# A fused attention and GeGLU kernel: one query group moved into the next block, a query/key group as half-tile pairs, padding copies ahead of the masks, a last PV ahead of its gates

## The chip, the cores and the metric

The kernel runs on one core of a Trainium2 chip. The metric is the device time of one execution in microseconds (us); less is better.

## The reference

With S = 2048 rows, D = 448, 16 heads of 28 and F = 1792, in bfloat16:

```
xn  = layernorm(x)                                   # no scale, no shift
q, k, v = split(xn @ wqkv)                           # 16 heads of 28
o   = softmax(q k^T / sqrt(28), window of 256, causal) v
out = x + o @ wo + (gelu(xn @ w_gate) * (xn @ w_up)) @ w_down
```

A query sees itself and the 255 rows ahead of it.

## The kernel before, in words

The rows are worked in four blocks (`qb` 0 to 3) of 512. The order of every engine is the order in which the program writes its instructions; no scheduler changes it. Eight PSUM banks are shared out by hand: four for scores or gates, four (`b0` to `b3`) that `take` hands out and `give` puts back, first in, first out.

**A block** has two stages. The attention stage is a list of score steps (nine in block 0, ten in the others, `steps_of`, L473). A step writes `sc` (L600), ScalarE turns it into `p_sb` by an exponential of 1.88 us (L604), the window is masked (by GpSimd selects, L528, in block 0; by VectorE products with the `masks` tile, L518, later), and TensorE meanwhile does the filler that `plan` lists for that step (L747 to L767). A filler entry `(u, 7)` advances the generator `u` seven times; `"sums"` and `"inverse"` put the softmax's denominators on VectorE, and `scale_o` (L537, GpSimd) multiplies by them. Every few steps `pv` (L562) multiplies the masked scores with `v_sb`, for the four head groups `g` 0 to 3 in turn; the last, `pv(3)`, is called by `rest` (L627). The second stage, `gated` (L422), does the gate products (`gt`), their Gelu, and the up products (`u`, or `ue` where they were made earlier). Its `last_v` is `rest`: so `pv(3)` stands behind gate 0. Its `hook` starts later work: norms and transposes of rows to come, `collect` and `deliver`.

**Projections.** `proj` and `qk_halves` (L229, L233) make q and k of a group as three products of 128 rows each and one of 64 rows each. `gen_pairs` (L311) makes them as seven pairs of 64-row products, two on the array at once; half of the operands then have to be in the other 64 partitions, which is what the copies `xsw` (from `xnT`) and `wsq` (from the padded weights `wqp` and `wkp`, L385) are for. Block 0's three later groups come from `gen_qk` (L259).

**Group 3 of k** has, for blocks 1 to 3, no products of its own. The 32 columns of a head leave four columns of padding, and `fill_pads` (L276) writes the weights of the last four k heads there, by small GpSimd copies. Group 3 of q comes from `q_last` (L249), four 128-row products. `collect` (L299) then sends the padding rows of `qT` and `kT` to DRAM by eight DMAs, and `deliver` (L306) reads them into `kT` by four.

**Queues.** Nearly all DMAs are issued by SP in program order; SP waits where the source is not ready, and everything behind it waits too. The start of its list: loads, `swap(0)` for `xsw` (L680), rows 8 to 11 of x (L681), then in `ahead` (L707) the transpose of row tile 4, the weights `wvs` and a slice of `wu`; in `ahead3` (L720) three more transposes, the `xsw` copies of block 1 and the remaining weights. The two `wsq` copies are issued by ScalarE in step 3 of block 0.

`make_masks` (L109) is 18 GpSimd selects. It stands before block 0's attention, `fill_pads(False)` in its step 2. The final stage is block 3's down product (`po`, L359) and the output.

Of the kernel before, what the change touches and what calls it, by code (L numbers as in the profile page):

```python
# [16 lines left out]
S, D, H, Dh, F = 2048, 448, 16, 28, 1792  # L17
P = 128
# [8 lines left out]
def kernel(  # L27
# [11 lines left out]
    nc = tc.nc  # L39
# [233 lines left out]
            qk_copies(0, g, pq, pk)  # L273
            yield 360

    def fill_pads(last):  # L276


        def put(dst, src, n, lo):

            src = src.rearrange("p (j d) -> p j d", d=Dh)[:, :, lo:]
            if n == 4:
                nc.gpsimd.tensor_copy(out=dst[:, 12:16, Dh:32], in_=src[:, :, 24:28])
            src = src[:, :, 0:24].rearrange("p j (g i) -> p g j i", i=8)[:, :, :, 0:4]
            nc.gpsimd.tensor_copy(out=dst[:, 0:12, Dh:32].rearrange("p (g j) i -> p g j i", j=4), in_=src)

        if not last:
            for c in range(3):
                k = wraw[:, c, D + 12 * Dh:2 * D]
                put(wqp[:, c, :, :], k, 4, 0)  # L290
                put(wkp[:, c, :, :], k, 3, 4)
            return
        put(w3p[0:64, :, :], w3k[0:64, :], 4, 0)
        put(w3p[64:128, :, :], w3k[64:128, :], 3, 4)
        nc.gpsimd.memset(w3p[64:128, 12:16, :], 0.0)

    k3 = dram.tile([4, 7, 4, QB], bf16, name="k3")
# [87 lines left out]
    def swap_weights():  # L385

        for hi, src in enumerate((wqp, wkp)):
            nc.scalar.dma_start(out=wsq[64 * hi:64 * hi + 64], in_=src[64 - 64 * hi:P - 64 * hi, 0:3])

    def xchunk(qb, hi, c, t0, n):  # L390

# [30 lines left out]
    def gated(qb, early, last_v, flush, hook):  # L422

        hT = hTs[qb]
        us, ges = {}, {}

        def up(p):
            if p in early:
                return
            us[p] = [take("u") for _ in range(2)]  # L430
            for c in range(7):
                chunk(us[p], wu, p, qb, c)

        def gate(p):
            gt = phase[0].pool.tile([P, 2, QB], f32, name="gt", tag="s")
            for c in range(7):
                chunk([gt[:, i, :] for i in range(2)], wg, p, qb, c)
            if not p:
                last_v()
            ges[p] = work.tile([P, 4, QB], bf16, name="p_sb", bufs=5)[:, 0:2, :]  # L440
            nc.scalar.activation(out=ges[p][:, :, :], in_=gt[:, :, :], func=ACT.Gelu_apprx_tanh)  # L441

        def end(p):
            ge = ges.pop(p)
            if p in early:
                nc.vector.tensor_tensor(out=both(hT, p), in0=ge[:, :, :], in1=both(hT, p), op=ALU.mult)
            else:
                for i, u in enumerate(us.pop(p)):
                    nc.vector.tensor_tensor(out=hT[:, p + 7 * i, :], in0=ge[:, i, :], in1=u, op=ALU.mult)  # L449
                    give(u)  # L450
                    flush()
            hook(2 * p)

        up(0)
        gate(0)
        end(0)
        gate(1)
        if 1 in early:
            end(1)
            gate(2)  # L460
            up(2)
        else:
            gate(2)
            up(1)
            end(1)
            up(2)
        end(2)
        for p in range(3, 7):
            gate(p)
            up(p)  # L470
            end(p)
# [59 lines left out]
    def attention(qb, plan):  # L531
# [4 lines left out]
        def scale_o(g, oc, inv):  # L536
            nc.gpsimd.tensor_tensor(out=oN[:, g, :], in0=oc[:, :], in1=inv, op=ALU.mult)  # L537
# [24 lines left out]
        def pv(g):  # L562

            ov = [take("ov") for _ in range(2 if qb else 1)]
            todo = parts.pop(g)
            for n, (half, kt, q0, nq, col, p_sb) in enumerate(todo):
                k0 = 64 * half if half else 0
                r = slice(k0, k0 + (P if half is None else 64))
                for j in range(4):
                    nc.tensor.matmul(ov[half or 0][32 * j:32 * j + 32, q0:q0 + nq], lhsT=v_sb[r, kt, 4 * g + j, :],  # L570
                                     rhs=p_sb[r, j, col:col + nq], start=n == (half or 0), stop=n + len(ov) >= len(todo),
                                     tile_position=(k0, 32 * j), skip_group_check=True)
            oc = work.tile([P, QB], f32, name="oc", tag="wb" if g % 2 else "wa", bufs=1)
            if qb:
                if g > 1:
                    behind.append((oc, ov))
                else:
                    add_halves(oc, ov)
            else:
                (nc.scalar.copy if g == 1 else nc.vector.tensor_copy)(out=oc[:, :], in_=ov[0][:, :])  # L580
                give(*ov)
            copied.append((g, oc))
# [3 lines left out]
        for i, (scores, ncol, edges) in enumerate(steps):  # L586
# [24 lines left out]
            while later:  # L611
                scale_o(*later.pop(0))
            for n in plan[i]:
                if n == "sums":
                    sums()
                elif n == "inverse":
                    inverse()
                if not isinstance(n, tuple):
                    if callable(n):
                        n()  # L620
                    continue
                for _ in range(n[1]):
                    next(n[0], None)
            if qb == 3 and i - 2 in pvs:
                inverse()

        def rest():  # L627
            while fresh:
                apply_masks(*fresh.pop(0))
            if not qb:  # L630
                scale_o(*later.pop(0))
                sums()
                inverse()
                scale_o(*later.pop(0))
            pv(3)

# [41 lines left out]
    transp(3, nc.vector.tensor_copy, "b3")  # L678
    pads(nc.scalar.copy, wkp, slice(0, 1))
    swap(0)  # L680
    nc.sync.dma_start(out=x_sb[:, 8:12, :], in_=xv[:, 8:12, :])  # L681
    pvs.append(take("pv", D))
    v_dense(1, pvs[1])
    pvs.append(take("pv", D, "b2"))
    pq, pk = (phase[0].pool.tile([P, 2, QB], f32, name="s0", tag="s")[:, 0, :] for _ in range(2))
    proj(pq, wqp, 0, 0)
    proj(pk, wkp, 0, 0)
    nc.vector.tensor_copy(out=w3p[:, :, 0:Dh], in_=wraw[:, 3, 0:D].rearrange("p (h d) -> p h d", d=Dh))
    nc.vector.memset(masks[:, 0, 0, 0:1], 1.0)
    make_masks()  # L690
    stat(4)
    rstd(4, 1)
    stat(5)
# [11 lines left out]
        pads(nc.vector.tensor_copy, dst, slice(2, 4))  # L705

    def ahead():  # L707
        norm(4)
        dma_transp(4)
        wv64 = A_wqkv[0:3 * P, 2 * D:3 * D].rearrange("(c h p) n -> h p c n", h=2, p=64)  # L710
        for hi in range(2):
            nc.sync.dma_start(out=wvs[64 * hi:64 * hi + 64, :, :], in_=wv64[1 - hi])
        load_ffn(wu, B_w_up, slice(0, 1))
# [6 lines left out]
    def ahead3():  # L720
# [2 lines left out]
            dma_transp(t)  # L723
        swap(1, 4, 2)
        swap(1, 6, 2)
        fill_pads(False)
        load_ffn(wg, B_w_gate, slice(0, 3))
        nc.sync.dma_start(out=x_sb[:, 12:16, :], in_=xv[:, 12:16, :])
        load_ffn(wu, B_w_up, slice(4, 7))
# [7 lines left out]
    for qb in range(NB):  # L737
# [4 lines left out]
        if qb == 0:  # L742
            new_hT(0)
            early = (0, 1, 2, 3)
            u = chain(gen_qk((1, 2, 3), {1: (3, pvs[3]), 2: (2, pvs[2])}), gen_up(0, (1, 2, 3, 0), (3,)))
            w = gen_pairs(1, (("v", 0), ("v", 2), ("k", 0), ("k", 1), ("k", 2)))
            plan = [[(u, 2), ahead, (u, 1)], [lambda: v_dense(2, pvs[2]), (u, 2), ahead2, (u, 1)],  # L747
                    [lambda: spare.append(spare.pop(1)), (u, 2), ahead3, (u, 4)], [swap_weights, lambda: stat(8), (u, 11)],
                    [lambda: stat(9), (u, 7), lambda: stat(10), (u, 7), lambda: fill_pads(True)], [(w, 7), "sums", "inverse"],
                    [(w, 11)], [lambda: stat(11), (w, 6), lambda: rstd(8, 4)],  # L750
                    [lambda: q_last(1, nc.vector.tensor_copy), (w, 4), "sums", "inverse", (w, 7)]]
        else:
            d = gen_down(qb - 1)
            if qb < 3:
# [3 lines left out]
                if qb == 1:  # L758
                    for i in range(4):
                        plan[i].insert(0, lambda t=12 + i: stat(t))  # L760
                    plan[4].append(lambda: rstd(12, 4))
            else:
                new_hT(3)
                early = (1, 2, 3, 4, 5, 6)
                u = gen_up(3, early)
                plan = [[(d, 14)], [(d, 4), (u, 5)], [(u, 9)], [(u, 7)], [(d, 18)], [(u, 7)], [(d, 13)], [(d, 5), (u, 7)],
                        [(u, 7)], [(d, 18)]]  # L767
        if qb in (1, 2):
            swap(qb + 1)
        score_pool(1)  # L770
        rest, after, flush = attention(qb, plan)
        nc.scalar.preload_act_table(ACT.Gelu_apprx_tanh)
        score_pool(2)
        if qb not in hTs:
# [1 line left out]

        def hook(f):
            after(f)
            if qb < 3 and f == 4:
                collect(qb + 1)  # L780
            if qb < 3 and f == 10:
                deliver(qb + 1)
            t = ({0: 8, 4: 9, 8: 10, 10: 11} if qb == 0 else {4: 12, 6: 13, 8: 14, 10: 15} if qb == 1 else {}).get(f)
            if t is not None:
                norm(t)
                dma_transp(t)
# [155 lines left out]
```

## Time and profile before

| | us |
|---|---|
| median of 3 runs | 217.1 |
| lowest and highest | 216.55, 217.58 |
| profiled execution, its own time | 216.48 |
| its span | 214.6 |
| TensorE busy in the span | 208.7 |
| VectorE, ScalarE, GpSimd busy | 159.8, 130.7, 46.4 |

The span runs from the first to the last instruction; 1.88 us of the execution's own time lie around it. Times within the trace are counted from the span's start. The granted TensorE clock is 1.0 in the whole span. The chain of waits follows the last instruction back to what released it; the time of a row in it is what that piece added to the chain, so neighbouring rows can be summed. In the timeline a row's time is that of the instructions themselves, which overlap on TensorE.

### The profile page before, as it was taken

What the parts mean: (1) busy time and instruction counts of PE and PEld (TensorE: products, weight loads), DVE (VectorE), ACT (ScalarE), POOL (GpSimd) and SP (SyncE); (2) the same over time, 40 slices, a digit from 0 to 9 for tenths busy, and PEclk for the clock granted to TensorE, in tenths of its full rate; (3) what the DMA queues carried; (4) which work ended last, traced back from release to release, by engine and by line L of the source; (5) the groups of instructions that cost most, each with busy time, mean ns of one, the idle gap of its engine ahead of it and who ended that gap; (6) DMA issues with size and microseconds to landing.
All of it is one profiled execution on the core that took longest, in us unless ns stands there. A gap on an engine that the chain in (4) does not pass through costs nothing.

```text
span 214.6 us, 6346 instructions
## 1 busy us (share of the span) xinstructions
PE 208.7 (97%) x2722; PEld 101.1 (47%) x2722; DVE 159.8 (74%) x355; ACT 130.7 (61%) x122; POOL 46.4 (22%) x78
## 2 busy tenths in 40 slices
PE   6999999999999999999999999999999999999993
PEld 2433444444444444444445436544444444444892
DVE  7899987997776995698546899576449699587621
ACT  4699599554877976523777897432678576466000
POOL 5287658630000211022000202022000021114001
PEclk9999999999999999999999999999999999999999
DMA  6998789993240001002230000200000000000011
GB/s 187 275 245 152 159 194 244 226 290 77 60 106 5 20 3 32 17 15 59 50 95 24 24 3 0 62 5 3 0 24 3 23 3 24 21 3 2 23 35 39
DMA packets 24193, 15.21 MB, mean 71 GB/s; under 512 B 9856, under 2 KB 24032, under 8 KB 24160
## 3 DMA queue, kind: packets, MB, share of 16 engines
q1 hardware_dynamic: 23056, 14.08, 28.3%
q10 hardware_dynamic: 1104, 0.68, 1.3%
q8 instruction: 22, 0.36, 0.8%
q14 instruction: 11, 0.09, 0.1%
HBM read 9.03 MB, written 2.18 MB: 52 GB/s over the span
## 4 chain that ended last, share of the span: by engine, by line
PE 94%; DVE 2%; ACT 1%; DMA 1%; issue 1%; DVEq 0%; ACTq 0%
PE po L359 26%; PE gt L401 20%; PE u L401 13%; PE ue L401 7%; PE sc L600 6%; PE pq L333 6%; PE ov L570 5%; PE pv L319 4%; PE pq L190 2%; PE pv L190 1%; DMA x_sb<-in_A_x_dram 1%; ACT p_sb L604 1%; DVE st L154 1%; PE s L190 1%; PE pk L190 1%
## 5 line engine op out<-in xcount | busy, mean ns | idle before, releaser
L604 ACT ACTIVATE p_sb<-sc 128x2048 bf16<-128x2048 f32 x39 | 73.3, 1878 | 20.6 <-PE sc L600 15.3
L441 ACT ACTIVATE p_sb<-gt 128x1024 bf16<-128x1024 f32 x28 | 28.6, 1023 | 39.5 <-PE gt L401 32.6
L537 POOL TENSOR_TENSOR oN<-oc,l 128x512 bf16<-128x512 f32 x16 | 22.3, 1391 | 137.8 <-DVE l L550 137.8
L359 PE MATMUL po<-wd,hT 128*128 128x448 bf16 (+1 forms) x266 | 47.9, 324 | 0.0
L401 PE MATMUL gt<-xnT,wg 64*128 64x512 bf16 x224 | 45.4, 376 | 0.0
L401 PE MATMUL gt<-xsw,wg 64*128 64x512 bf16 x168 | 40.6, 376 | 0.0
L449 DVE TENSOR_TENSOR hT<-p_sb,u 128x512 bf16<-128x512 bf16 x36 | 23.3, 680 | 19.6 <-PE u L401 11.9
L518 DVE TENSOR_TENSOR p_sb<-p_sb,masks 128x256 bf16<-128x256 bf16 (+1 forms) x90 | 30.2, 389 | 5.0 <-ACT p_sb L604 5.0
L359 PEld LDWEIGHTS <-hT 128*128 128x128 bf16 x266 | 24.6, 98 | 16.0 <-issue 1.4
L401 PE MATMUL u<-xnT,wu 64*128 64x512 bf16 x144 | 29.9, 376 | 0.0
L401 PEld LDWEIGHTS <-wg 64*128 64x128 bf16 x392 | 19.3, 94 | 22.2 <-issue 0.2
L401 PEld LDWEIGHTS <-wu 64*128 64x128 bf16 x392 | 18.6, 94 | 23.2 <-issue 3.1
L401 PE MATMUL u<-xsw,wu 64*128 64x512 bf16 x108 | 26.1, 376 | 0.0
L367 DVE TENSOR_TENSOR res<-po,x_sb 128x448 bf16<-128x448 f32 (+1 forms) x17 | 10.1, 593 | 17.3 <-PE po L359 17.3
L401 PE MATMUL ue<-xnT,wu 64*128 64x512 bf16 x80 | 16.6, 377 | 0.0
L600 PE MATMUL sc<-qT,kT 28*64 28x320 bf16 (+7 forms) x648 | 16.4, 261 | 0.1
L528 POOL TENSOR_SCALAR_AFFINE_SELECT p_sb<-p_sb 128x512 bf16<-128x512 bf16 (+1 forms) x21 | 14.2, 701 | 6.5 <-ACT p_sb L604 6.4
L359 PE MATMUL po<-wo,oN 128*128 128x448 bf16 (+1 forms) x76 | 15.1, 323 | 0.0
L401 PE MATMUL ue<-xsw,wu 64*128 64x512 bf16 x60 | 14.9, 377 | 0.0
L600 PEld LDWEIGHTS <-kT 28*64 28x64 bf16 (+1 forms) x648 | 7.5, 102 | 12.6 <-issue 11.0
L418 DVE CAST hT<-ue 128x512 bf16<-128x512 f32 x19 | 12.1, 679 | 0.5 <-PE ue L401 0.4
L570 PE MATMUL ov<-p_sb,v_sb 64*32 64x320 bf16 (+7 forms) x648 | 11.7, 256 | 0.1
(103 smaller groups left out, 265.6 us busy)
## 6 DMA issues: line engine op xcount, KB each, us to landing
out_dram<-res SPq DMA_DIRECT2D x15, 112.0 KB
wd<-in_B_w_down_dram SPq DMA_DIRECT2D x2, 784.0 KB
x_sb<-in_A_x_dram SPq DMA_DIRECT2D x3, 448.0 KB
wu<-in_B_w_up_dram SPq DMA_DIRECT2D x4, 336.0 KB
xsw<-xnT SPq DMA_DIRECT2D x6, 192.0 KB
wg<-in_B_w_gate_dram SPq DMA_DIRECT2D x2, 448.0 KB
wg<-in_B_w_gate_dram SPq DMA_DIRECT2D x2, 336.0 KB
wraw<-in_A_wqkv_dram SPq DMA_DIRECT2D x2, 252.0 KB
```

The costliest lines, as they stand in the source:

```text
L333: nc.tensor.matmul(ps, lhsT=w.rearrange("p h d -> p (h d)"), rhs=xchunk(qb, hi, c, qb * QB, QB), start=c == 0, stop=c == 6, tile_position= ...
L359: nc.tensor.matmul(po[:, a:b], lhsT=x[:, k, cs], rhs=wt[:, k, lo + a:lo + b], start=(n == a == 0), stop=(n == len(terms) - 1), skip_group_ ...
L401: nc.tensor.matmul(ps, lhsT=w[64 * hi:64 * hi + 64, c, p * P:(p + 1) * P], rhs=xchunk(qb, hi, c, qb * QB, QB), start=c == 0, stop=c == 6, ...
L418: copy(out=hTs[qb][:, p + 7 * i, :], in_=us[i])
L441: nc.scalar.activation(out=ges[p][:, :, :], in_=gt[:, :, :], func=ACT.Gelu_apprx_tanh)
L449: nc.vector.tensor_tensor(out=hT[:, p + 7 * i, :], in0=ge[:, i, :], in1=u, op=ALU.mult)
L518: nc.vector.tensor_tensor(out=reg, in0=reg, in1=m, op=ALU.mult)
L528: nc.gpsimd.affine_select(out=reg, in_=reg, pattern=mid + [[1 if diag else -1, min(w, P)]], compare_op=ALU.is_ge, fill=0.0, base=0 if diag ...
L537: nc.gpsimd.tensor_tensor(out=oN[:, g, :], in0=oc[:, :], in1=inv, op=ALU.mult)
L570: nc.tensor.matmul(ov[half or 0][32 * j:32 * j + 32, q0:q0 + nq], lhsT=v_sb[r, kt, 4 * g + j, :], rhs=p_sb[r, j, col:col + nq], start=n == ...
L600: nc.tensor.matmul(ss[k0:k0 + nk, j, col:col + nq], lhsT=kT[r, g, kt * P + k0:kt * P + k0 + nk], rhs=qT[r, g, ring(qb).start + q0:ring(qb) ...
L604: nc.scalar.activation(out=p_sb[:, :, 0:ncol], in_=ss[:, :, 0:ncol], func=ACT.Exp, scale=SCALE)
```

## The change

Four edits, which share tiles and queues.

- Block 1's fourth group of q (`q_last(1)`) leaves the last step of block 0 and stands in step 1 of block 1, ahead of eight down products; step 1 has three down products less than before and step 2 three more. `collect(1)` and `deliver(1)` leave block 0's gates for the ends of steps 2 and 4 of block 1.
- Block 0's fourth group of q and k is made by `gen_pairs` in step 2, and no longer by `gen_qk`. So `wsq` is needed in step 2: `swap_weights` moves to the head of `ahead`, in step 0, and to SP's queue, and rows 8 to 11 of x move behind the transpose of tile 4.
- The padding copies are split by group (15 copies for 9) and stand before and behind the first projection; the three copies for `w3p` stay (`fill_last`). `make_masks` moves to block 0's gates, and a VectorE memset of one column of `masks` goes.
- In block 3 `rest` is called before the gates, so `pv(3)` is ahead of `u` 0 and gate 0. The last step's masks and group 1's `inverse` are put before the last down product of step 9; group 2's two halves are added at once and not behind the exponential.

```diff
-    def fill_pads(last):
...
+    def put(dst, src, n, lo, gs):
+        src = src.rearrange("p (j d) -> p j d", d=Dh)[:, :, lo:]
+        if n == 4 and gs.stop == 4:
+            nc.gpsimd.tensor_copy(out=dst[:, 12:16, Dh:32], in_=src[:, :, 24:28])
+        a, b = gs.start, min(gs.stop, 3)
+        src = src[:, :, 8 * a:8 * b].rearrange("p j (g i) -> p g j i", i=8)[:, :, :, 0:4]
+        nc.gpsimd.tensor_copy(out=dst[:, 4 * a:4 * b, Dh:32].rearrange("p (g j) i -> p g j i", j=4), in_=src)
+    def fill_pads(gs):
+        for c in range(3):
+            k = wraw[:, c, D + 12 * Dh:2 * D]
+            put(wqp[:, c, :, :], k, 4, 0, gs)
+            put(wkp[:, c, :, :], k, 3, 4, gs)
...
     def swap_weights():
         for hi, src in enumerate((wqp, wkp)):
-            nc.scalar.dma_start(out=wsq[64 * hi:64 * hi + 64], in_=src[64 - 64 * hi:P - 64 * hi, 0:3])
+            nc.sync.dma_start(out=wsq[64 * hi:64 * hi + 64], in_=src[64 - 64 * hi:P - 64 * hi, 0:3])
...
-            if not p:
+            if not p and qb < 3:
                 last_v()
...
-                if g > 1:
+                if g > 1 + qb // 3:
                     behind.append((oc, ov))
...
-            if qb == 3 and i - 2 in pvs:
+            if qb == 3 and pvs.get(i - 2) == 0:
                 inverse()
...
     swap(0)
-    nc.sync.dma_start(out=x_sb[:, 8:12, :], in_=xv[:, 8:12, :])
...
+    fill_pads(slice(1, 4))
     proj(pq, wqp, 0, 0)
     proj(pk, wkp, 0, 0)
     nc.vector.tensor_copy(out=w3p[:, :, 0:Dh], in_=wraw[:, 3, 0:D].rearrange("p (h d) -> p h d", d=Dh))
-    nc.vector.memset(masks[:, 0, 0, 0:1], 1.0)
-    make_masks()
+    fill_pads(slice(0, 1))
...
     def ahead():
+        swap_weights()
         norm(4)
         dma_transp(4)
+        nc.sync.dma_start(out=x_sb[:, 8:12, :], in_=xv[:, 8:12, :])
...
-        fill_pads(False)
...
-            u = chain(gen_qk((1, 2, 3), {1: (3, pvs[3]), 2: (2, pvs[2])}), gen_up(0, (1, 2, 3, 0), (3,)))
+            u = chain(gen_qk((1, 2), {1: (3, pvs[3]), 2: (2, pvs[2])}), gen_pairs(0, (("k", 3),)), gen_up(0, (1, 2, 3, 0), (3,)))
...
-                    [lambda: spare.append(spare.pop(1)), (u, 2), ahead3, (u, 4)], [swap_weights, lambda: stat(8), (u, 11)],
+                    [lambda: spare.append(spare.pop(1)), ahead3, (u, 10)], [lambda: stat(8), (u, 11)],
...
-                    [lambda: q_last(1, nc.vector.tensor_copy), (w, 4), "sums", "inverse", (w, 7)]]
+                    [(w, 4), "sums", "inverse", (w, 7)]]
...
+                    plan[1] = plan[1][:1] + [lambda: q_last(1, nc.vector.tensor_copy), (d, 8)]
+                    plan[2] = plan[2][:1] + [(d, 14), lambda: collect(1)]
+                    plan[4].append(lambda: deliver(1))
...
-                        [(u, 7)], [(d, 18)]]
+                        [(u, 7)], [(d, 17), "masks", "inverse", (d, 1)]]
...
+        if qb == 3:
+            rest()
...
+            if qb == 0 and f == 6:
+                make_masks()
-            if qb < 3 and f == 4:
+            if qb in (1, 2) and f == 4:
                 collect(qb + 1)
-            if qb < 3 and f == 10:
+            if qb in (1, 2) and f == 10:
                 deliver(qb + 1)
```

More of the change, by code (lines that the diff above doesn't have):

```diff
@@ L274, in gen_qk, with fill_last @@
             yield 360
-    def fill_pads(last):
[L279 to L294, printed above, removed]
+    def put(dst, src, n, lo, gs):
[10 more added lines that the diff above has]
+            put(wkp[:, c, :, :], k, 3, 4, gs)
+    def fill_last():
+        put(w3p[0:64, :, :], w3k[0:64, :], 4, 0, slice(0, 4))
+        put(w3p[64:128, :, :], w3k[64:128, :], 3, 4, slice(0, 4))
         nc.gpsimd.memset(w3p[64:128, 12:16, :], 0.0)
@@ L613, in attention @@
             for n in plan[i]:
-                if n == "sums":
+                if n == "masks":
+                    apply_masks(*fresh.pop(0))
+                elif n == "sums":
                     sums()
@@ L633, in rest @@
                 inverse()
+                scale_o(*later.pop(0))
+            while later:
                 scale_o(*later.pop(0))
@@ L744 @@
             early = (0, 1, 2, 3)
-            u = chain(gen_qk((1, 2, 3), {1: (3, pvs[3]), 2: (2, pvs[2])}), gen_up(0, (1, 2, 3, 0), (3,)))
+            u = chain(gen_qk((1, 2), {1: (3, pvs[3]), 2: (2, pvs[2])}), gen_pairs(0, (("k", 3),)), gen_up(0, (1, 2, 3, 0), (3,)))
             w = gen_pairs(1, (("v", 0), ("v", 2), ("k", 0), ("k", 1), ("k", 2)))
             plan = [[(u, 2), ahead, (u, 1)], [lambda: v_dense(2, pvs[2]), (u, 2), ahead2, (u, 1)],
-                    [lambda: spare.append(spare.pop(1)), (u, 2), ahead3, (u, 4)], [swap_weights, lambda: stat(8), (u, 11)],
-                    [lambda: stat(9), (u, 7), lambda: stat(10), (u, 7), lambda: fill_pads(True)], [(w, 7), "sums", "inverse"],
+                    [lambda: spare.append(spare.pop(1)), ahead3, (u, 10)], [lambda: stat(8), (u, 11)],
+                    [lambda: stat(9), (u, 7), lambda: stat(10), (u, 7), fill_last], [(w, 7), "sums", "inverse"],
                     [(w, 11)], [lambda: stat(11), (w, 6), lambda: rstd(8, 4)],
-                    [lambda: q_last(1, nc.vector.tensor_copy), (w, 4), "sums", "inverse", (w, 7)]]
+                    [(w, 4), "sums", "inverse", (w, 7)]]
         else:
```

## The prediction

> **What bounds the kernel now.** I read the page's busy times first, then the table by stage, then the chain of waits, then the timeline of each engine where the change cuts. The page:
>
> ```profile
> PE 208.7 (97%) x2722; PEld 101.1 (47%) x2722; DVE 159.8 (74%) x355; ACT 130.7 (61%) x122; POOL 46.4 (22%) x78
> ...
> PE 94%; DVE 2%; ACT 1%; DMA 1%; issue 1%; DVEq 0%; ACTq 0%
> ```
>
> TensorE is the bound and the chain is nearly all TensorE. By stage (columns: length, busy time of each engine):
>
> ```profile
> 11.64:53.50 41.86, 41.61 (x444) 17.42 (x443) 37.71 (x77) 30.08 (x30) 23.85 (x47) 1.00 0.93 198
> 53.50:82.00 28.50, 28.50 (x486) 13.79 (x486) 23.65 (x57) 23.09 (x20) 2.54 (x2) 1.00 0.15 37
> ```
>
> Look at length against the first busy time: TensorE is idle 0.25 us from block 0's first scores to block 1, and never after that until the output. So no stall can be removed that is worth over 0.25 us; the change can gain only TensorE's own work, and every new wait of TensorE is paid in full. The DMA share of 0.93 in that stage (next to last column) says that a transfer put earlier there has to queue.
>
> **What the edits save on TensorE.** In the chain, a run of full 128-row products ahead of or behind 64-row pairs carries about 0.1 us more than its products:
>
> ```profile
> 17.28 0.75 PE pq L190 x3
> 18.03 0.65 PE pk L190 x3
> 18.68 0.32 PE pq L196
> ...
> 34.39 0.75 PE pq L190 x3
> 35.14 0.22 PE pq L253
> 35.36 0.32 PE pq L333
> 35.68 0.21 PE pq L333
> ...
> 57.11 2.20 PE po L359 x11
> ...
> 76.48 0.75 PE pq L190 x3
> 77.24 0.22 PE pq L253
> 77.45 0.95 PE po L359 x5
> ```
>
> (a) *Block 0's fourth q/k.* Removed: 0.75 + 0.65 + 0.32 = 1.72. Added: seven pairs. 28 products of that form in a row take 3.13 in the chain and 22 take 2.48, so a pair is 0.65 / 3 = 0.217 and the entry 2.48 - 11 x 0.217 = 0.09; seven pairs with entry are 1.61. The up products behind need no entry in either case. Saved 0.11.
>
> (b) *Block 1's fourth q.* Removed from block 0: 0.75 + 0.22 = 0.97; the pair behind it keeps its entry (0.32 against 0.21), since it then follows scores. Added in block 1: the same 0.97, but the down products behind it start without an entry: at 77.45 five cost 0.95, 0.19 each, while eleven behind scores cost 2.20, that is 2.09 + 0.11. Added 0.86, saved 0.11. The down products only change their step.
>
> (c) *Block 3's last PV.* Now: up 0 at 1.62, gate 0 at 1.51, PV 0.66, six gates 9.18, sum 12.97. Then: PV behind down products 0.68 (as at 78.40), up 0 1.62, gate 0 1.51, six gates without entry 6 x 1.51 = 9.06; sum 12.87. Saved 0.10.
>
> Together 0.32 us. The page "TensorEngine Tiling (Array Packing)", Key Properties, in the Trainium skill says that a change of tiling mode drains TensorE; by the rows above that drain is the 0.1 us entry.
>
> **What the edits make TensorE wait for.**
>
> (d) *A bank that is not free: the largest term.* In step 2 of block 0 the pool hands out the two banks that came back first, the second of which held group 2's q; ScalarE empties it:
>
> ```profile
> 16.99 0.58 ACT L243 CAST qT<-pq 128x512 bf16<-128x512 f32 x1
> ...
> 22.20 0.52 ACTq L388 DMA_DIRECT2D wsq<-wqp  x1
> 22.89 0.48 ACTq L388 DMA_DIRECT2D wsq<-wkp  x1
> ```
>
> Now the fourth group's q comes first, and its k (which gets that bank) starts at 17.87 in TensorE's timeline: the copy, done at 17.57, is hidden. As a pair, q and k start together at 17.21, and the k half must wait for 17.57 plus about 0.06 (TensorE starts 0.06 behind VectorE's `xnT` copy at 8.97). Seven k products from 17.63 instead of 17.23: +0.40. Queued behind the waiting product is all of TensorE. Nothing ahead of that copy on ScalarE changes (exponential to 16.40, two small operations on statistics that end at 16.47). Bounds: 0 if the copy came 0.4 earlier, 0.6 if the copy itself is as late again by a third. I take 0.40.
>
> (e) *`wsq` in time.* It has to be there at 17.6 by (d), no longer at 30.5. Before it can be issued: the wraw load, the GpSimd copies, VectorE's copies into `wqp` and `wkp` (end 13.05). By the sizes of the issues the wraw rest is the last of 2.18 MB; the page's slices move 1.0 and 1.48 MB by 10.7, so it lands between 9.6 and 10.7. Nine padding copies took 1.39 us at 20.6, 0.155 each; 15 from 10.5 end at 12.9, all within the time in which the 18 mask selects stand now (9.25 to 14.30), so GpSimd's first p_sb select is not later. SP is free from 11.28. The first copy goes out at about 13.0 and the second at 13.6. Landing: the queue of the two copies above has two packets left in the DMA view of 25.3 to 26.0, so the second took 2.4 to 3.1 us from its issue. Near end 16.0, with time to spare. Far end: the `xsw` copies ahead of it (second issued at 10.65) land, by 3.2 MB issued against 3.79 moved at 16.1 us, at 13.7 to 14.7, up to 4.1 from issue; with pads 0.9 late (below) that is 14.5 + 4.1 = 18.6. I take 16.3 and 0 us; at the far end 1.0 us.
>
> SP's other work behind it: the transpose of tile 4 moves from 13.60 to some 14.4, and rows 8 to 11, `wvs` and `wu` end near 18.9 against a transpose that starts at 18.65 now: 0.2 to 0.3 later. The first `xsw` copies of block 1 follow; their packets end at about 26.1 by the DMA view, needed at 26.8, where TensorE is 0.3 later too: 0. ScalarE loses two issues and the DMA queues lose `wsq` at 23 to 25, which helps them.
>
> (f) *A cover that is used up.* Block 0's last PV waits for GpSimd's selects of the last step. GpSimd's row, then TensorE's:
>
> ```profile
> 36.45 1.82 POOL L528 TENSOR_SCALAR_AFFINE_SELECT p_sb<-p_sb 128x512 bf16<-128x512 bf16 x3 [0.82 <-ACT p_sb L604]
> ```
> ```profile
> 39.28 0.68 PE L570 MATMUL ov<-p_sb,v_sb 128*32 128x128 bf16 x20
> ```
>
> The cover is 39.28 - 38.27 = 1.01, and (b) takes 0.97 of it away: +0.03 with a wake of 0.06, between 0 and 0.15. Also group 2's pair of block 1 now comes 0.97 sooner on a bank that VectorE empties until 35.17 (L580, late because GpSimd holds `oc` to 34.45): +0.03, 0 to 0.1.
>
> (g) *Block 3's end.* PV needs the last masks: exponential 180.83 to 182.71, masks 0.82 more, against 184.1: in time. Then `inverse` (0.70) stands ahead of the last `res` on VectorE, 183.5 to 184.2, so `res` ends at about 184.85; up 0 takes that bank as its second at 184.85: +0.05, 0 to 0.3. The half sum of group 2 (0.69) fits into ScalarE's idle 0.82 and VectorE's wait. Its scale moves behind the last masks, which then no longer stretch (1.86 against 0.82, below).
>
> (h) *`collect` and `deliver` in block 1.* SP is idle there. Eight issues from 62.3 (2.7 us, as at 83.62), then `deliver` behind the output of tile 2 (`res` ends at 68.85): four issues 69.2 to 71.0, the last at 70.6, landing at 73.0 to 73.7 if it takes the 2.4 to 3.1 of the second `wsq` copy, which moved seven times its bytes; needed at 73.4. I take 0; far end 0.3. VectorE's 0.69 copy moves with (b); `make_masks` (5.05 us) runs beside gates from some 46.7, where GpSimd has nothing else, and ends at 51.8, ahead of its first use at about 55.3.
>
> **Sum:** -0.32 + 0.40 + 0.06 + 0.05 = +0.19. The profiled execution's own time is 216.48, so 216.7; it lay 0.62 under the median of the runs shown, from which the same sum gives 217.3. I forecast between them: **216.9 us**. Within 0.5% (1.1 us) counts as no change; about that can be told from none here.
>
> **Rivals.** *Bank free in time* (d falls out): ScalarE's copy would have to end at 17.2. Then -0.2: 216.3 to 216.9. For it: only 0.4 us decide. Against: its row and the unchanged work ahead. Chance 0.16. The same time results if one of the small waits turns out covered and a pair is cheaper.
>
> *`wsq` late*: slower than before. Place: step 2, the k half's first product. It decides from a landing after 17.6; at the far end of 18.6 it costs 1.0 on top: 217.7 from the profiled execution, 218.3 from the median. For it: DMA share 0.93 and a wait chain over four engines. Against: the plain reading has 1.3 us to spare. Chance 0.15.
>
> *Padding copies collide with VectorE.* GpSimd's L537 beside the masks stretches them:
>
> ```profile
> 178.89 0.82 DVE L518 TENSOR_TENSOR p_sb<-p_sb,masks 128x256 bf16<-128x256 bf16 x3
> ...
> 181.49 1.86 DVE L518 TENSOR_TENSOR p_sb<-p_sb,masks 128x256 bf16<-128x256 bf16 x3
> ```
>
> But VectorE's four weight copies ran beside the mask selects without that (0.26 at 11.50, 0.27 at 7.82 with GpSimd idle). If padding copies act like L537, each of the four waits up to a padding copy of 0.22: 0.9 in all, 0.3 of it ahead of group 1's k at 12.63. Time 217.0 to 217.2. Chance 0.09. The page "SBUF — State Buffer" of the Trainium skill has VectorE and GpSimd share a port pair under an exclusive lock; the trace agrees for L537 and not for the selects.
>
> **Chances.** Forecast 0.60, bank free 0.16, `wsq` late 0.15, collision 0.09. Slower by over 0.5%: most of `wsq` late and a little of the rest, 0.17; faster by over 0.5%: only if the bank is free and the runs fall low, 0.08; within: 0.75. Range 216.0 to 218.0: from bank free to the far end of `wsq`.
>
> **What would show it.** (a) to (c): no product above 0.22 behind step 2's pairs, down products at 0.19 behind the moved q. (d): a gap of 0.4 on TensorE in step 2 that ends with ScalarE's copy. (e): a gap that ends later, with a DMA. (f): PV starts as the third select ends. Wrong if TensorE's busy time falls by another amount than 0.3, or a gap over 0.2 stands elsewhere.

## The result and the profile after

The changed kernel takes 217.76 us (median; 216.97 to 218.83, 22 runs), the kernel before 216.81 us beside it (216.05 to 217.63, 22 runs). The ratio is 1.0047, with a 95% interval of 1.0032 to 1.0062: slower by 0.95 us at the medians, where the sum of the prediction had +0.19. (Its 216.9 us stood beside the three runs with a median of 217.1; beside 216.81 the sum gives 217.0.) Runs over 1.5% above the fastest of their kernel (219.33 of e1, 220.59 of e5 below) stand in the medians but not in the ratios. The profiled execution of the changed kernel is one of its longer ones: 218.48 us, span 216.7, that is 2.1 above the span of before. So the profile shows more loss than the median has, and the experiments must say which part is always there.

The page of the changed kernel, busy times and chain:

```profile
PE 209.8 (97%) x2728; PEld 106.5 (49%) x2728; DVE 159.9 (74%) x354; ACT 130.8 (60%) x122; POOL 47.8 (22%) x84
...
PE 81%; DMA 10%; DVE 3%; SPq 3%; issue 1%; ACT 0%; DVEq 0%
```

In the chain DMA rises from 1% to 10%: what ended last now runs through transfers. The table by stage, in the stretches of before:

```profile
11.64:53.50 41.86, 39.96 (x435) 16.75 (x436) 37.24 (x76) 28.85 (x28) 26.40 (x57) 1.00 0.98 194
53.50:82.00 28.50, 28.50 (x490) 13.62 (x487) 22.50 (x56) 22.12 (x19) 1.42 (x2) 1.00 0.16 41
```

Length less the first busy time: TensorE is idle 1.90 us in the first stretch, where it was 0.25; in the second nothing, as before. TensorE's timeline has both places:

```profile
17.24 0.39 PE L334 MATMUL pq<-xnT,wqp 64*128 64x512 bf16 x1
18.50 0.39 PE L334 MATMUL pk<-xsw,wsq 64*128 64x512 bf16 x1 [0.87 <-DMA wsq<-wkp]
...
42.77 0.80 PE L402 MATMUL gt<-xnT,wg 64*128 64x512 bf16 x4
44.33 0.39 PE L402 MATMUL gt<-xsw,wg 64*128 64x512 bf16 x2 [0.76 <-DMA wg<-in_B_w_gate_dram]
```

The first q product of the new pairs starts at 17.24 and the next product of either half only at 18.50. That is step 2 of block 0. The second gap, in front of gate 3, is one of which the prediction says nothing. And the chain, where the three terms of TensorE's own work can be checked:

```profile
13.75 4.71 DMA wsq<-wkp
18.50 0.39 PE pk L334
...
30.67 13.61 DMA wg<-in_B_w_gate_dram
44.33 3.19 PE gt L402 x27
...
58.53 0.77 PE pq L190 x3
59.30 0.22 PE pq L253
59.52 1.51 PE po L360 x8
...
186.45 0.66 PE ov L571 x40
187.11 1.73 PE u L402 x14
188.84 10.58 PE gt L402 x98
199.41 13.88 PE po L360 x126
```

**A ledger.** Scores stand at the same places in both programs, so their starts can be compared step by step. The columns give by how much a stretch of TensorE's work is longer than in the profiled execution of before: A is step 2 of block 0 (from its scores to step 3's), B from block 0's last scores to block 1's first (the moved q is worth -0.97), C steps 1 and 2 of block 1 (where it now stands).

| kernel | A | B | C | span |
|---|---|---|---|---|
| forecast | +0.29 | -0.91 | +0.86 | |
| changed kernel | +1.15 | +0.18 | +0.86 | 216.7 |
| the same again (e4) | +1.16 | -0.97 | +0.86 | 215.6 |

So A is 0.86 over the forecast in both executions, and B is 1.1 over it in one and not in the other. C is as forecast.

### The profile page after: what moved, and what is told of

Its sections match the earlier page's. It is cut to its first block, busy times and chain, and to the rows that moved or that the text cites. A ratio compares the mean times of both kernels' runs of the same rounds, so it can differ in the third digit from the quotient of the medians.

```text
span 216.7 us, 6375 instructions
## 1 busy us (share of the span) xinstructions
PE 209.8 (97%) x2728; PEld 106.5 (49%) x2728; DVE 159.9 (74%) x354; ACT 130.8 (60%) x122; POOL 47.8 (22%) x84
## 4 chain that ended last, share of the span: by engine, by line
PE 81%; DMA 10%; DVE 3%; SPq 3%; issue 1%; ACT 0%; DVEq 0%
PE po L360 26%; PE gt L402 18%; PE u L402 13%; DMA wg<-in_B_w_gate_dram 6%; PE ue L402 5%; PE sc L601 5%; PE pq L334 4%; PE ov L571 4%; PE pv L320 3%; DMA wsq<-wkp 2%; SPq L81 1%; SPq L383 1%; DMA x_sb<-in_A_x_dram 1%; PE pq L190 1%; PE pk L334 1%
## 5 line engine op out<-in xcount | busy, mean ns | idle before, releaser
L402 PE MATMUL gt<-xsw,wg 64*128 64x512 bf16 x168 | 38.7, 376 | 0.8 <-DMA wg<-in_B_w_gate_dram 0.8
L402 PEld LDWEIGHTS <-wg 64*128 64x128 bf16 x392 | 23.9, 94 | 19.1 <-DMA wg<-in_B_w_gate_dram 1.3
L519 DVE TENSOR_TENSOR p_sb<-p_sb,masks 128x256 bf16<-128x256 bf16 (+1 forms) x90 | 29.2, 380 | 5.1 <-ACT p_sb L605 5.1
L402 PEld LDWEIGHTS <-wu 64*128 64x128 bf16 x392 | 19.5, 94 | 22.6 <-issue 2.7
L402 PE MATMUL u<-xsw,wu 64*128 64x512 bf16 x108 | 25.0, 376 | 0.0
L368 DVE TENSOR_TENSOR res<-po,x_sb 128x448 bf16<-128x448 f32 (+1 forms) x17 | 10.1, 593 | 17.7 <-PE po L360 17.6
L601 PE MATMUL sc<-qT,kT 28*64 28x320 bf16 (+7 forms) x648 | 16.4, 261 | 0.1
L334 PE MATMUL pk<-xsw,wsq 64*128 64x512 bf16 x30 | 11.3, 377 | 0.9 <-DMA wsq<-wkp 0.9
```

The source lines that it names most:

```text
L334: nc.tensor.matmul(ps, lhsT=w.rearrange("p h d -> p (h d)"), rhs=xchunk(qb, hi, c, qb * QB, QB), start=c == 0, stop=c == 6, tile_position= ...
L368: nc.vector.tensor_tensor(out=res[:, 0:w], in0=po[:, 0:w], in1=x_sb[:, t, lo:up], op=ALU.add)
L402: nc.tensor.matmul(ps, lhsT=w[64 * hi:64 * hi + 64, c, p * P:(p + 1) * P], rhs=xchunk(qb, hi, c, qb * QB, QB), start=c == 0, stop=c == 6, ...
L519: nc.vector.tensor_tensor(out=reg, in0=reg, in1=m, op=ALU.mult)
L601: nc.tensor.matmul(ss[k0:k0 + nk, j, col:col + nq], lhsT=kT[r, g, kt * P + k0:kt * P + k0 + nk], rhs=qT[r, g, ring(qb).start + q0:ring(qb) ...
```

## The experiments

Theory one (W in the expectations): `wsq` is late in step 2, and its price is 0.85 us on top of the bank's 0.40. Theory two (Q): the gates of block 0, which start 0.97 earlier since the q has left, catch up with the load of `wg`, whose arrival the change does not move. The rivals are the prediction's: the bank, and the padding copies. Kernels of one table share the chip and the runs of before. The edited kernels and e4 have 12 runs each, e9 to e12 have 6; before has 35, 35 and 11.

| kernel | median (lowest, highest) | ratio to before, 95% |
|---|---|---|
| before | 216.69 (216.05, 217.36) | |
| e1 q/k as full products | 217.01 (216.07, 219.33) | 0.9997 to 1.0045 |
| e2 pairs behind two up products | 216.89 (216.55, 217.84) | 0.9999 to 1.0029 |
| e3 no `wsq` in block 0 | 217.00 (216.35, 217.89) | 1.0010 to 1.0039 |
| e4 the same again | 217.54 (216.59, 218.33) | 1.0024 to 1.0057 |

| kernel | median (lowest, highest) | ratio to before, 95% |
|---|---|---|
| before | 216.69 (216.14, 217.46) | |
| e5 transpose later | 216.87 (216.42, 220.59) | 0.9997 to 1.0042 |
| e6 only the moved q | 217.67 (216.14, 218.58) | 1.0012 to 1.0059 |
| e7 `wg` first | 217.46 (217.03, 218.93) | 1.0029 to 1.0065 |
| e8 pairs later, `wg` first | 216.67 (216.51, 217.29) | 0.9990 to 1.0013 |

| kernel | median (lowest, highest) | ratio to before, 95% |
|---|---|---|
| before | 216.89 (216.37, 217.56) | |
| e9 only the last PV | 216.66 (216.52, 216.93) | 0.9972 to 1.0008 |
| e10 before, `wg` first | 216.66 (216.43, 216.89) | 0.9970 to 1.0005 |
| e11 q, PV and `wg` first | 216.50 (216.15, 216.74) | 0.9961 to 0.9997 |
| e12 all mended | 216.72 (216.46, 217.23) | 0.9975 to 1.0014 |

### e1: the fourth q/k as full products again

From the changed kernel:

```diff
-gen_qk((1, 2), ...), gen_pairs(0, (("k", 3),)), gen_up(...)
+gen_qk((1, 2, 3), ...), gen_up(...)
-                    [lambda: spare.append(spare.pop(1)), ahead3, (u, 10)], ...
+                    [lambda: spare.append(spare.pop(1)), (u, 2), ahead3, (u, 4)], ...
```

> The changed kernel with the fourth q/k group of block 0 made by full 128-row products again, wsq and the order of SP's queue as changed. Theory W (the wait for wsq in step 2 is the loss): the 1.26 us gap at 17.24 goes and 0.1 of products comes back, so 1.1 to 1.2 under the changed kernel, 0.2 under the kernel before. Theory Q (the new order of the DMA queue makes a later load late, wg at gate 3, 1.1 us in the changed profile): the gap at gate 3 stays and the time is at most 0.3 under the changed kernel. Both can hold in part.

A is 0.00: without the pairs nothing is lost in step 2, though the padding copies stand where the change put them. B is -0.47 and not -0.97. In the waits of this kernel (columns: us in total, times, longest) half a microsecond of gate 3 is named:

```profile
PEld L402 <- DMA wg<-in_B_w_gate_dram: 0.6, 1, 0.6
```

So the wait at gate 3 does not need the pairs. Its runs spread from 216.07 to 219.33, and the interval holds 1: by the median alone this run decides nothing.

### e2: the pairs behind two up products

```diff
-gen_pairs(0, (("k", 3),)), gen_up(0, (1, 2, 3, 0), (3,))
+gen_up(0, (1, 2), (3,)), gen_pairs(0, (("k", 3),)), gen_up(0, (3, 0), (3,))
```

> The changed kernel with the half-tile pair put behind two of block 0's four early up products, some 3 us later. Theory W: neither wsq (landed 18.45) nor the bank is waited for, the pair keeps its 0.1: 1.2 to 1.3 under the changed kernel, 0.3 under the kernel before. Theory Q: the gap at gate 3 stays, gain under 0.3.

The `wsq` wait is gone, yet A is +0.42: an up product takes the bank in the pair's place and waits for the same copy of ScalarE. The next step loses 0.33 more. The forecast (0.3 under the kernel before) missed. TensorE's timeline:

```profile
17.67 0.39 PE L402 MATMUL ue<-xsw,wu 64*128 64x512 bf16 x2 [0.16 <-ACT qT L243]
...
23.05 0.68 PE L571 MATMUL ov<-p_sb,v_sb 128*32 128x128 bf16 x20 [0.26 <-DVE hT L419]
```

Whoever comes first on that bank pays, and the later pairs push a PV onto a bank that VectorE empties. B is +0.05: in this execution 1.0 us was lost at gate 3.

### e3: the pairs of block 0 without `wsq`

```diff
-... if c % 2 == hi else wsq[r, c // 2, hs, :]
+... if c % 2 == hi or not qb else wsq[r, c // 2, hs, :]
```

> The changed kernel, but the fourth pair of block 0 reads wqp and wkp where it should read wsq, so it waits for no copy; those products are of the wrong rows. Forecast of the prediction for what then is left: a gap of 0.40 that ends with ScalarE's copy of group 2's q at 17.6. Theory W: 0.8 to 0.9 under the changed kernel. If no gap is left in step 2, the bank term of the prediction was wrong; if the time does not fall, theory Q.

The pairs read `wqp` and `wkp` where the copies are meant, so products of the right rows are left out and nothing waits for `wsq`. A is +0.29, which is 0.40 - 0.11 to the hundredth: the k half starts at 17.68, by the bank alone. So 0.86 of A's 1.15 is `wsq` and nothing else, and the bank's term has its forecast size. The median is 217.00, against 217.54 with the wait: 0.54 less, and not 0.86, since without this wait the gates come earlier and can meet the other one.

### e4: the changed kernel again

No edit.

> The changed kernel once more, for a second profile. Theory W: the gap in step 2 is there again, ends with wsq, 1.0 to 1.3 us. Theory Q: the gap at gate 3 is there again, 0.8 us or more. If one of the two gaps is missing here, it is not what the median lost.

A is +1.16 again, B is -0.97. The `wsq` wait is in both executions; the wait for `wg` comes and goes.

### e5: the transpose of tile 4 behind the loads

```diff
         norm(4)
-        dma_transp(4)
         nc.sync.dma_start(out=x_sb[:, 8:12, :], in_=xv[:, 8:12, :])
...
         load_ffn(wu, B_w_up, slice(0, 1))
+        dma_transp(4)
```

> The changed kernel with the DMA transpose of row tile 4 moved behind the loads of rows 8 to 11, wvs and the wu slice. In both profiles of the changed kernel the last wsq bytes move at 16.3 and TensorE goes on at 18.5. If the transpose queued behind wsq holds back its completion, the gap in step 2 now ends at 17.6 to 17.7 with ScalarE's copy (the bank term), 0.8 less. If wsq completes late by itself, the gap stays at 1.2. Either way the wait for wg at gate 3 can come or not.

The `wsq` copies and their order stay; only what stands behind them in SP's queue changes. SP's timeline in the changed kernel (issue and its length):

```profile
13.09 0.48 SPq L389 DMA_DIRECT2D wsq<-wqp  x1
13.75 0.48 SPq L389 DMA_DIRECT2D wsq<-wkp  x1
14.32 1.34 SPq L175 DMA_TRANSPOSE xnT<-xn  x1
15.72 0.56 SPq L715 DMA_DIRECT2D x_sb<-in_A_x_dram  x1
```

and in e5:

```profile
13.18 0.48 SPq L389 DMA_DIRECT2D wsq<-wqp  x1
13.84 0.48 SPq L389 DMA_DIRECT2D wsq<-wkp  x1
14.38 0.58 SPq L714 DMA_DIRECT2D x_sb<-in_A_x_dram  x1
...
18.41 2.67 SPq L175 DMA_TRANSPOSE xnT<-xn  x2
```

The copies are issued 0.09 later, and the wait for them is gone; TensorE in e5:

```profile
16.96 0.40 PE L601 MATMUL sc<-qT,kT 28*128 28x128 bf16 x8
17.29 0.39 PE L334 MATMUL pq<-xnT,wqp 64*128 64x512 bf16 x1
17.70 0.37 PE L334 MATMUL pk<-xsw,wsq 64*128 64x512 bf16 x1
```

A is +0.29, as without `wsq`. What held the copies? The DMA view of 13 to 19 us, GB/s in slices of 0.15 us, first of the changed kernel, then of e5:

```profile
GB/s 194 239 246 212 171 171 130 82 273 273 191 253 143 266 184 389 430 205 143 185 114 171 225 185 80 27 48 0 0 3 13 16 9 10 10 248 382 329 143 376
```
```profile
GB/s 231 294 212 212 225 198 178 96 137 232 239 178 266 184 184 144 410 389 307 68 223 233 167 197 221 245 311 346 364 347 317 329 317 365 346 233 266 175 244 183
```

Count to the 26th figure of the first row (27): from 16.75 to 18.25 no slice is over 48, and TensorE goes on at 18.50; in the same slices of e5 none is under 245. By the packets in the trace the last bytes of `wsq` had been written at 16.24 (at 16.16 in e5). What was late is the word that they were there: ten packets of four bytes that began at 16.4 to 16.9 took 1.4 to 1.83 us each. (The trace has such packets behind the data of the copies; I read them as the notice.) e4 has eight such, e5 none. The semaphore, the counter on which TensorE waits, says it outright. It gets 16 updates from the `wkp` copy: in the changed kernel one at 16.55 and fifteen at 18.31 to 18.45, in e5 all at 16.31 to 16.82. From issue to last update this copy takes 4.3 to 4.7 us in the seven profiled executions with the transpose right behind it (4.70 in the changed kernel) and 2.9 to 3.0 in the two without (e5, e12). So the transpose queued behind the copies holds their completion; how it does so isn't shown. That the copies also moved from ScalarE's queue to SP's, where the transpose is, was not tried apart; from ScalarE's queue, in before, the same copy takes 3.22. An instruction fetch of 16 KB falls into the same time, but e5 has one between 13 and 19 us too, and has a stretch under 50 GB/s of its own, 20.8 to 21.7, behind its own transposes, with no fetch beside it.

### e6: only the moved q, on the kernel before

```diff
-                    [lambda: q_last(1, nc.vector.tensor_copy), (w, 4), "sums", "inverse", (w, 7)]]
+                    [(w, 4), "sums", "inverse", (w, 7)]]
...
+                    plan[1] = plan[1][:1] + [lambda: q_last(1, nc.vector.tensor_copy), (d, 8)]
+                    plan[2] = plan[2][:1] + [(d, 14), lambda: collect(1)]
+                    plan[4].append(lambda: deliver(1))
...
-            if qb < 3 and f == 4:
+            if qb in (1, 2) and f == 4:
...
-            if qb < 3 and f == 10:
+            if qb in (1, 2) and f == 10:
```

> The kernel before with one edit alone: block 1's fourth q moved into block 1, with collect and deliver. The prediction's sum: 0.11 less, less 0.06 of used-up cover, so 216.6. Theory Q, now stated as: the gates of block 0 come 0.97 earlier against a load stream that does not, and gate 3 needs wg; without the change TensorE is at gate 3 at 42.9 and the last bytes of wg move at 41.95. Then TensorE waits 0 to 0.9 at gate 3, and the time is 0 to 0.8 over the kernel before.

Four runs lie at 216.14 to 216.39, eight at 217.10 to 218.58: the edit that was to save 0.11 loses 0.35% by the ratio (interval 0.12 to 0.59%). The profiled execution is of the lower group (216.39); A is 0.00, B -0.77, C +0.87, and 0.2 is lost in front of gate 3 already there. The upper group was not profiled.

### e7: `wg` ahead of the last `wu` and of rows 12 to 15

From the changed kernel, in `ahead3`:

```diff
         load_ffn(wg, B_w_gate, slice(0, 3))
-        nc.sync.dma_start(out=x_sb[:, 12:16, :], in_=xv[:, 12:16, :])
-        load_ffn(wu, B_w_up, slice(4, 7))
         load_ffn(wg, B_w_gate, slice(3, 7))
+        load_ffn(wu, B_w_up, slice(4, 7))
...
+        nc.sync.dma_start(out=x_sb[:, 12:16, :], in_=xv[:, 12:16, :])
```

> The changed kernel with wg's pairs 3 to 6 loaded ahead of wu's, and rows 12 to 15 of x behind wd. wg then comes some 5 us earlier. Theory Q: no wait at gate 3 any more, up 4 takes its wu in time, 0.3 to 0.6 under the changed kernel on the median. Theory W: the gap of 1.2 in step 2 stays, so still 0.3 to 0.6 over the kernel before.

B is -0.97, with no wait for `wg`; its last packets end at 37.98 and not at 43.32. The kernel gains nothing (1.0047; e4 1.0041), where 0.3 to 0.6 was forecast: A (+1.33) is untouched, and the profiled execution, one of the longer ones (218.36), shows a third weak place. TensorE, then GpSimd:

```profile
13.24 0.39 PE L190 MATMUL pq<-xnT,wqp 128*128 128x512 bf16 x1 [0.26 <-POOL wqp L283]
```
```profile
11.75 0.20 POOL L280 COPY wqp<-wraw 128x16 bf16<-128x16 bf16 x1 [8.09 <-DMA wraw<-in_A_wqkv_dram]
```

The padding copies now stand in front of the first q products and wait for the wraw load; where it is late (11.75 here, 10.86 in the changed kernel's profile), step 0 loses time: 0.64 here.

### e8: e2 and e7 together

```diff
+gen_up(0, (1, 2), (3,)), gen_pairs(0, (("k", 3),)), gen_up(0, (3, 0), (3,))
...
+        load_ffn(wg, B_w_gate, slice(3, 7))
+        load_ffn(wu, B_w_up, slice(4, 7))
```

> The changed kernel with both: the pair behind two up products and wg first. If W and Q are all that the change lost, neither gap is left and the time is 0.2 to 0.3 under the kernel before. If a third loss exists, it stays at or over the kernel before.

Neither wait is left: A is +0.29 and the next step +0.25 (the banks), B -0.97. Eleven of the 12 runs lie between 216.51 and 216.99; the tail of e2, 217.27 to 217.84 in five of 12 runs, is gone. With both waits away the change as a whole loses nothing: 1.0001 (0.9990 to 1.0013) against 1.0041 (1.0024 to 1.0057) for e4. It doesn't gain the forecast 0.2 to 0.3 either; the banks still cost what A and the next step show.

### e9: only the last PV ahead of the gates, on the kernel before

```diff
-            if not p:
+            if not p and qb < 3:
                 last_v()
...
-                        [(u, 7)], [(d, 18)]]
+                        [(u, 7)], [(d, 17), "masks", "inverse", (d, 1)]]
...
+        if qb == 3:
+            rest()
```

> The kernel before with the last edit alone: block 3's last PV ahead of its gates, masks and inverse in step 9. Prediction: 0.10 less on TensorE's products and 0.05 of wait on the bank of the last res: 0.05 less, which these runs cannot tell from nothing; in the profile the way from step 9's scores to the first of the last down products is 0.05 to 0.1 shorter than the 16.9 of the kernel before. It adds nothing to theories W and Q.

From the last scores to the last down products 16.83 us, 16.84 in before: this edit is worth 0.01. Its chain says why:

```profile
184.64 0.66 PE ov L570 x40
185.30 1.73 PE u L401 x14
187.02 10.58 PE gt L401 x98
```

The gates are 7 x 1.51 with no entry, as forecast, but `u` 0 takes 1.73 and not 1.62. VectorE's `res` ends at 185.30, and the second half of `u` 0 starts at 185.35, 0.11 behind the first. Up to block 3 this kernel is the one before, and still its scores are 0.46 later, 0.15 before the first scores and 0.30 at block 0's step 5, where the waits name an `xsw` copy: such is the spread between two executions. At that step the other profiles of this chip lose 0.57 (e10), 0.15 (e11) and 0.45 us (e12), those of the other chips at most 0.10: a fourth place at which a transfer decides.

### e10: before, with the loads of e7's order

```diff
+        load_ffn(wg, B_w_gate, slice(3, 7))
+        load_ffn(wu, B_w_up, slice(4, 7))
```

> The kernel before with wg's pairs 3 to 6 loaded ahead of wu's and rows 12 to 15 of x behind wd, nothing else: a control. Theory Q: the kernel before has about 0.9 of cover at gate 3 in its profile, so little changes on the median, 0 to 0.2 less, and its slow end (217.4) falls if some of its runs wait for wg.

216.66, and the interval holds 1. The order of the loads alone is no gain that can be told from none, as long as no gate comes early.

### e11: e6, e9 and the order of the loads, on the kernel before

```diff
+                    plan[1] = plan[1][:1] + [lambda: q_last(1, nc.vector.tensor_copy), (d, 8)]
...
+        load_ffn(wg, B_w_gate, slice(3, 7))
+        load_ffn(wu, B_w_up, slice(4, 7))
...
+        if qb == 3:
+            rest()
```

> The kernel before with the moved q, the last PV ahead of the gates and the new order of loads; full products for block 0's fourth group, masks and padding as before. Theory Q: no wait for wg, so 0.11 + 0.10 - 0.06 - 0.05 = 0.1 under the kernel before on the median, and no runs over 217.3. If runs at 217.5 and over come back, another wait than wg made them.

The fastest of all, 216.50, below before by 0.03 to 0.39%; all runs are under 216.75. B is -0.94 and C +0.86, so the moved q saves 0.07 in this profile; the rest of the 0.39 us at the median goes, as far as can be argued, with the longer executions of before, which e11 does not have. The loss of e6 is thereby one of the loads: 1.0035 with their old order, 0.9979 with the new.

### e12: the changed kernel with three repairs

```diff
-        dma_transp(4)
...
         load_ffn(wu, B_w_up, slice(0, 1))
+        dma_transp(4)
...
+        load_ffn(wg, B_w_gate, slice(3, 7))
+        load_ffn(wu, B_w_up, slice(4, 7))
...
-                    [lambda: spare.append(spare.pop(1)), ahead3, (u, 10)], ...
+                    [ahead3, (u, 10)], ...
```

> The changed kernel with its pair where it is, the transpose of tile 4 behind the loads, wg first, and the pool of banks not turned before step 2, so that the k half gets a bank that VectorE empties at 17.4. Wait in step 2 then 0.2 where it was 0.4 (bank) and 1.2 (wsq); no wait at gate 3. Sum -0.32 + 0.22 + 0.06 + 0.05 = 0.0 against the kernel before. If a gap of 0.4 or more is left in step 2, the bank is not what ended it.

The third repair gives the pairs another bank. TensorE's timeline of step 2:

```profile
17.55 0.39 PE L334 MATMUL pq<-xnT,wqp 64*128 64x512 bf16 x1
17.79 0.37 PE L334 MATMUL pk<-xsw,wsq 64*128 64x512 bf16 x1
```

k follows q at 0.24, though ScalarE ends its copy of group 2's q only at 18.05: so it was that bank that cost 0.40. The other bank held v, and VectorE empties it until 17.73, so A is still +0.11 and not -0.11; step 0 loses 0.20 more to padding copies that begin at 11.52. 216.72 is no different from before, and not better than e11: the pairs of block 0 never earned their 0.11.

## Why the prediction was wrong, by its own steps

**(e) failed, in the landing of the second `wsq` copy.** The issues were forecast to 0.15 us (13.0 and 13.6; they are 13.09 and 13.75) and the last bytes to 0.06 (16.3; 16.24). But the forecast took the last packet of a copy for its end, while TensorE waits for the notice behind it. That alone would have cost nothing: in before the last byte is written at 25.36 and the last semaphore update comes at 26.11, 3.22 us from the issue, and 13.75 + 3.22 = 16.97 is still ahead of 17.6. What failed is that the landing time was carried over from a place where no transpose stands right behind the copy. The prediction itself puts the transpose of tile 4 there, at some 14.4, and counts only its own delay, not what it does to the copy ahead of it: the last update came at 18.45, 4.70 us from the issue and 2.2 us behind the last byte. The far end, 18.6 and 1.0 us, was the right case: TensorE goes on at 18.50, 0.86 for it. The rival "`wsq` late" with a chance of 0.15 was the one that happened; its condition (a landing after 17.6) and its price held, its reason (a chain over four engines, a crowded DMA) did not: the chain was on time, and so were the bytes.

The Trainium skill, "DMA: Bandwidth & Descriptors", section "Anatomy of one DMA", gives a fixed cost of about 2.0 us, most of it the receipt of the last byte (told there for DMAs issued by GpSimd). That would be a rival to the transpose. The runs speak against it: in e5 the last byte is written at 16.16 and the product starts at 17.70, held by the bank alone, and the last semaphore update came at 16.82, 0.66 us behind the byte; and at gate 3 TensorE goes on 0.8 to 1.0 us behind the last `wg` packet (41.40 and 42.21 in e6, 43.32 and 44.33 in the changed kernel).

**(b) was sized rightly and lacked a wait.** -0.97 in block 0 and +0.86 in block 1 came out to the hundredth. The prediction weighed what the earlier end of block 0 does to the last PV and to group 2's bank, (f), but not to the gates behind. In before the last `wg` packet ends at 41.95 and the last of the load's 16 semaphore updates comes at 42.87; gate 3 starts at 42.92:

```profile
42.92 0.59 PE L401 MATMUL gt<-xsw,wg 64*128 64x512 bf16 x2
```

That is 0.05 of cover, and none for 0.97. That e6 alone loses, that e7, e8, e11 and e12 wait no more, and that the wait changes from execution to execution (0 in e4, 0.2 in e6, 0.5 in e1, 1.0 in e2, 1.15 in the changed kernel) all agree. The prediction's "wrong if a gap over 0.2 stands elsewhere" is this gap. In the changed kernel itself A's loss puts the cover back: its gates come 0.27 later than in before, and it waits only because its last `wg` packet is 1.37 later in that execution (its last update comes at 44.29, and TensorE goes on at 44.33); e4, with the packet at 41.92 and the last update at 42.87, does not wait. So the median's loss is that of `wsq` above all: A, B and C of e4 sum to +1.05, and 0.95 was measured (0.85 in e4's own runs). The second wait is what keeps kernels without the first (e3, e5) from being faster; that is argued from the ledgers, since their longer executions were not profiled.

**(a) and (d) held**: e3 and e5 give their sum, +0.29, and no entry of the up products stands in the way. ScalarE's row is the one that was forecast to within 0.04:

```profile
17.02 0.59 ACT L243 CAST qT<-pq 128x512 bf16<-128x512 f32 x1
```

e12 shows that it was the bank. "Bank free in time" did not happen. **(c) and (g)**: -0.10 and +0.05 were forecast, -0.01 is measured; the PV costs 0.66 for 0.68, and (g) is 0.11 for 0.05, within its bounds. **(f)**: 0 for 0.06, by B of e4 and e5 (-0.97, forecast -0.91). **(h)**: no wait in block 1. **"Padding copies collide"** did not happen: with the copies running beside them from 10.86 to 13.2, VectorE's four weight copies took 0.27, 0.27, 0.37 and 0.40 us, beside 0.26, 0.26, 0.37 and 0.37 in before. But their wait for the load (e7, e12) is a cost that no step had.

Put together with the measured sizes: -0.11 (a), -0.11 (b), -0.01 (c, g), +0.40 (d), +0.86 (e), a total of +1.03. The forecast's line was -0.11, -0.11, -0.05, +0.40, 0 for (e) and +0.06 for (f), that is +0.19. The range of 216.0 to 218.0 holds 217.76 only because it was drawn to the far end of `wsq`. One of the prediction's signs can't be read: TensorE's busy time was to fall by 0.3 and the page has 209.8 for 208.7, but e10, with the products of before, has 209.5.

## What to carry to other kernels

A transfer is in time when its notice arrives, not when its last packet does: leave about a microsecond for it (0.7 to 1.0 us here where nothing held it), and look at what is queued right behind it, a transpose above all. Work taken out of a full engine makes everything behind it come earlier, so each load that is needed later has to be measured against its new time, up to the next place where the two programs meet again. And where a wait varies between executions, one profile shows it or doesn't: profile the same kernel twice, and read its list of times for two groups.

## What the runs showed of the hardware

- A DMA transpose issued 0.57 us behind a copy held that copy's completion to 2.2 us past its last byte, and in that time all transfers of the core came almost to a stop for 1.5 us (under 50 GB/s from 16.75 to 18.25). With other loads in its place (e5) the completion comes 0.66 us behind the last byte, and the traffic stays at 245 GB/s or more. In before the same transpose, issued at 13.60, brings only a dip (85 GB/s in one slice); what makes the difference stays open.
- The last `wg` packets end between 40.8 and 43.3 in the nine profiled executions that have the old order of loads, and between 36.2 and 38.0 in the five with `wg` first. Nine tenths of these packets have ended by 39.3 to 40.5 in the former; what delays the last of them was not tried separately. The semaphore shows that it is one share in sixteen: in those nine, fifteen of the load's 16 updates have come by 41.05 to 42.36, the last one 0.5 to 2.7 us later. The three loads ahead of it on the queue have the same lag within an execution: 2.7 to 2.9 us in the changed kernel, 1.1 to 1.2 in before.
